# The first batch's q and k loaded by pairs of heads, and the global keys moved to the end of a key tile

## The chip, the cores and the metric

The kernel runs on one core of a Trainium2 chip. The metric is the time of one execution on the device in microseconds (us). Five engines work side by side, each through its own list of instructions in order: PE (matrix multiply, with its weight loads), DVE (vector), ACT (scalar, with tables for exp and sine), POOL (which here builds masks and issues most loads) and SP (which only issues DMAs). Semaphores tie the lists together. Results of PE land in PSUM, eight banks of 128 partitions by 512 f32, and DVE or ACT must carry them out before a bank is used again.

## The reference

Two layers, one after the other, on 4 batches of 768 positions, 8 heads of 64.

```python
scores = scale * np.matmul(q, k.transpose(0, 1, 3, 2))
is_global = pos[None, :] < 8
is_local = (rel >= 0) & (rel < 96)            # rel = query position - key position
dist = np.where(is_global & ~is_local, 96.0, np.abs(rel))
scores = np.where(is_global | is_local, scores - slopes[h] * dist, -1e9)
x = softmax(scores) @ v                        # heads side by side: 768 x 512 for each batch
proj = x @ w_proj                              # 512 -> 1536: x1, x2, x3
y = x1 * irfft(rfft(x2) * filter_fft) * x3     # along the 768 positions
out = y @ w_out
```

So a query sees the 95 keys before it, itself, and the first 8 keys of the sequence.

## The kernel before

**Tiles.** Keys go in tiles of 112 (`KL`), with the 8 global keys beside them so that one 128-row matmul gives both. Before the change a tile has 128 rows: 0 to 7 hold the global keys, 8 to 15 nothing, 16 to 127 the 112 local ones (`LO` is 16). Seven tiles cover 768 positions; the last starts at 656 and repeats 16 keys of the sixth. A tile of keys is multiplied with the 208 queries that can see it (96 for the last). The seven tiles are worked in three groups (`GRP`): two, two and three. Heads are taken in pairs (`hp` 0 to 3), one on partitions 0 to 63 and one on 64 to 127.

**Attention of a batch** (`attention`, L900 on). q and k come by DMA with positions on the partitions (`load_rows`, `load_q`: one head's 64 values make a packet of 256 bytes, cast to f16 on the way). PE turns them (`turned`, L668), DVE or ACT copies them out to `QT` and `KT`, `global_keys` copies the 8 global columns into every tile. Then, for each group and pair: `scores` (PE, L711), exp (ACT, L739), the mask (DVE, L751). In batch 0 the distance bias is instead added by PE (`biases`, L698: small matmuls with `slope` and `dg`, `near`, `edge`), so that no mask is needed. `values` (PE, L769 and L774) multiplies with V, which has a column of ones for the sum; DVE takes the reciprocal (L799) and scales (`xn`, L793); PE turns `xn` (L815) to `xT`. For groups 1 and 2 of batch 3 the turns are DMA transposes on SP (`crossed`, L657).

**Second layer.** `gate` (L860) makes x1 and x3; the butterflies and `conv` (L934, L622, L959) project and do the transform along positions with small tables in three classes; L986 is the output projection, then L310 or L312 and a store on SP. The tables come from a sine pass of ACT (`tables`, L424), which needs the sine table loaded and the exp table loaded again behind it. `spectrum` (L558 on) prepares the filter.

**The start.** q tiles 0 to 2 and k tile 0 are loaded as f32 by SP and ACT (`first_tiles`) and turned as f32 (`turned32`, L635). The other tiles of batch 0 come by POOL's queue, one DMA for a tile: k, q, then V (`load_first`). The 16 global rows of V of batch 0 are a small load of their own, copied by DVE into the seven tiles (`first_rows`). PE first runs idle matmuls (L302) on zeros.

**What sets the order.** Every operation of the program is an `Op` with the engines that may do it. The string `ORDER` at the top is the schedule, written out: `83P2` is operation 83 on PE with its result in bank 2, `74A` operation 74 on ACT, `i17b0` seventeen idle matmuls in bank 0. Each engine gets its instructions in the order of the string, and the string also decides whether DVE or ACT does a copy. Nothing is rearranged at run time; an engine that waits holds up all behind it.

Of the kernel before, what the change touches and what calls it, by code (L numbers as in the profile page):

```python
# [9 lines left out]
F32 = mybir.dt.float32  # L10
# [7 lines left out]
NG = 8  # L18
# [22 lines left out]
4V 0S 1A 2S 3A 30V 9G 32A 31A 14V 13V 11V 10A 33V 22G 34V 23V 60A 62A 12V 27V 5V 65A 36G 39G 19S 35A 15V 25V 24G 63A  # L41
16V 40G 18V 42G 41G 59A 45G 28V 8V 26V 46G 48G 29A 47G i17b0 74P0 75V 61A 70P1 72P2 71V 68P3 69V 84P45 64A 106P0 76P1
37G 58A 92P67 73A 79A 78A 93P 88P23 77V 94P 85P 38G 108P1 89P 49G 86P 107A 66V 90P 95A 44G 43G 109V 112P0 113V 87A
110P1 111V 80P67 81P 82P 20V 91A 51G 67V 120P01 83A 114P45 121A 152P2 153V 50G 154P3 155V 118P67 158P0 115A 159V 119A
156P2 157V 17V 116P45 21V 117A 160P67 161A 162P23 163A 96P45 97V 98V 101P01 166P67 167A 164P45 122P23 52G 102V 103V
123V 127P01 104P6 124V 128V 53G 129V 7G 217P7 165A 105A 99P4 168P23 125P6 130P5 258G 100V 218A 126A 212P4 131A 173P01
137P5 132P6 169V 170V 171P2 213A 219V 220V 221A 174V 175V 176P7 138P3 259G 172A 357P0 214V 215V 133P2 134A 267G 266G
216A 224P6 177V 199V 198V 206V 139V 385P7 184P4 358A 55G 135V 255G 189P5 140A 141V 386V 179P7 225A 257G 355P3 256G
264G 226A 183P0 265G 359A 6A 353P1 191A 201V 143P5 227V 181A 136V 194P7 56G 57G 185A 200V 202V 356V 383P0 228V 229A
205V 260G 186A 354V 208V 230A 223V 361P23 145A 203V 196A 367P45 362A 364P67 384V 178P1 207V 148P0 365A 295P2 204V 360V  # L50
368A 180V 396P45 150A 296A 397A 390P67 209V 210V 211V 187V 363V 370P01 371A 391A 293P3 294A 270G 369V 291P2 280P0 366V
387P67 222V 292A 398V 388A 231V 232V 233V 234V 393P45 299P3 300A 394A 54G 281A 282P2 283A 429P1 273G 306P3 307A 278P6
279A 147P7 149A 286P2 372V 261S 235V 236V 272G 287A 389V 142P3 433P6 434A 271G 431P7 144A 263G 430A 485G 237V 373P45
262S 151V 268G 297P2 298A 240P6 484G 241A 182V 193P3 195A 374V 432V 238P2 239A 392V 243P6 244A 269G 375V 395V 378P01
486G 379V 380V 435P45 436A 487G 197V 438P23 439A 404P67 405V 146V 376P0 496G 406V 245P1 246A 377V 437V 581P4 284P5
285A 444P23 445A 441P67 442A 407P1 188P0 488G 582V 399P45 381P2 408A 440V 585P3 274G 190V 400V 401V 446V 583P0 382A
586V 252P67 254A 253A 275G 276G 495G 584V 402P1 403A 447P45 489G 490S 443V 613P7 614A 248P23 448V 494G 587A 249A 304P6
305A 452P01 410P7 250A 412A 500G 247V 712G 449V 450P2 453V 454V 425P6 451A 251V 501G 455P3 659P7 456V 502G 427A 493G
302V 660A 595P01 589P45 498G 478V 590A 596A 592P23 593A 588A 414P6 458P7 499G 727G 468P4 416A 301V 661P5 308V 711G
460A 303V 242V 729G 594V 409P0 657P1 658V 611P2 309V 288V 612A 289V 424P6 426A 428V 477V 479V 290V 411A 470A 662A  # L60
473P1 475A 420P7 422A 415P6 413V 312P4 480V 313A 320P5 725G 417A 324P1 472P0 321V 474A 669P23 325A 598P67 599A 523P4
481V 714G 510P1 670A 316P5 314P0 192V 511A 600V 672P23 621P67 317V 524A 715G 482V 812P1 315A 591V 673A 322P4 323A 622A
310P0 311A 813V 730G 814A 418V 419P5 318P1 319A 597V 506P4 507A 421V 491S 463P5 465A 624P67 618P01 619A 666P23 457P4
667A 519P5 674V 625A 483V 508P0 663P23 881S 615P67 713G 326V 327V 328V 329V 623V 330V 520A 664A 462P1 423V 509A 620V
720G 728G 497G 616A 521P5 492G 606P23 505G 333V 334V 464A 467P0 469A 522A 607V 601P67 466V 277G 602V 608V 459A 626V
350P1 810P5 514P0 665V 351A 716G 347P4 603A 503G 835S 671V 525P1 526A 348A 476V 344P2 717S 722G 811V 837S 504G 527P5
345A 515A 528A 617V 668V 632P67 331V 604P4 605A 678P23 532P0 633V 634V 533A 679V 512P5 513A 680V 332V 808P1 627P67
628V 882S 534P0 675P45 676V 609P2 809A 629V 535A 610A 635P1 335P3 677V 630P2 631V 529V 636A 721G 836S 471V 336A 724G
530V 883S 821P01 822A 818P67 819A 820V 815P45 816A 726G 880S 723G 838S 516V 338P3 839V 652P2 654A 681S 339A 642P6 644A
817V 648P7 531V 846P45 517V 682S 840P23 683S 650A 847A 518V 823V 824P01 825A 826V 647P6 841A 643P7 645A 638P4 640A  # L70
719G 827P01 828V 884V 341P5 829V 342A 649A 646V 653P7 849P01 850A 536V 732G 537V 461V 651V 705V 891P45 343S 892A
888P23 704V 851V 637P6 544P0 689P1 707V 639A 655A 545A 548P4 731G 691A 549A 550P6 542P5 893V 842V 540P7 543A 706V 352S
538P0 539A 552P1 553A 695P4 551A 641V 700P0 541A 702A 708V 697A 690P1 830P67 546P0 692A 848V 685P4 684P1 831V 832V
889A 687A 843P23 693V 890V 709V 885P67 340S 547A 844A 894P45 733P0 895A 886A 554V 710V 896V 718S 750P2 855P45 856V
748P3 735P6 337S 686A 656V 857V 751A 845V 833S 834S 887V 555A 556V 699P2 736A 557V 734A 749A 852P45 853V 900P67 901V
897P01 349S 902A 854V 898V 899V 694P3 558V 737P4 754P5 746P0 738A 741P4 858S 755A 561V 747A 562V 752P1 903S 753A 742A
739P5 559V 560V 759P0 760A 761P6 762A 346S 757V 763V 740A 743V 859S 575P1 576A 701A 572P4 573A 696A 578P0 566P1 764V
904S 703V 871P2 756V 865P3 867A 563P4 564A 758V 771P3 767P5 567A 579A 861P6 772A 863A 744V 860P4 745V 769P7 779P3 780A
905S 765P6 775P0 768A 927V 773P1 926V 929V 688V 862A 928V 776A 568S 930V 931V 777P3 770A 778A 698V 937P5 569P4 766A
932V 774A 781V 782V 783V 946P7 784V 785V 933P6 947A 938A 935P7 936A 961P5 570A 948P3 941P7 949A 934A 786V 950P4 787V  # L80
788V 951A 939P3 906P6 942A 940A 571S 952P4 944V 959P7 960A 943V 577S 945V 954P1 955A 864V 870P3 962A 963V 875P7 964V
907P1 909A 953A 580S 957V 956V 916P5 917P0 919A 876P4 873A 908A 958V 872A 874V 790P1 877V 565S 791A 965P6 866P2 966A
969P3 970V 971P6 878A 879V 868A 789V 972A 574S 984P4 985A 967P7 978P2 968A 973V 980P6 981A 982P4 983A 918V 920V 793P7
869V 910V 796P6 979A 986V 922P2 974A 975V 797A 987A 921P3 799P6 800A 801S 923A 976V 977V 798S 794A 802P4 988V 805P6
991V 989V 795S 911P7 992V 912P3 924A 806A 990V 993V 925V 807S 792S 994V 1004V 1001P6 803A 913A 1006V 804S 914V 998P7
999A 1000S 915V 1007V 995P3 1005V 1011P7 1002A 1003S 1012V 996A 997S 1008P6 1014P3 1015A 1009V 1013S 1010S 1016S
"""


# [108 lines left out]

class Fused:
    PERIOD = 40.0  # L200
    NEAR = 3
    PAIR_X = ()
    PAIR_AB = ()
    PAIR_EO = ()
# [1044 lines left out]
```

## Time and profile before

| what | us |
|---|---|
| median of 3 runs (lowest to highest) | 169.65 (169.21 to 169.74) |
| profiled execution | 168.69 |
| its span | 166.8 |
| PE, DVE, ACT, POOL busy | 160.3, 152.9, 144.9, 73.6 |
| PE: idle matmuls | 1.19 to 7.68 |
| first exponential / last of batch 0 ends | 11.63 / 22.28 |
| first matmul with V | 18.51 |
| sine table load | 25.49 |
| first gate / first projection of the second layer | 25.39 / 37.53 |
| end of the last stretch of matmuls on the chain | 160.69 |

How to read it: times are from the start of the span of one profiled execution. The profile gives busy time of each engine, the time it sat idle and what ended that, and a chain of waits that is followed back from the last instruction. Matmuls overlap, so a busy PE can still have room: the spacing of their starts tells what they cost. A DVE or ACT instruction in a row of others also starts some 0.07 to 0.1 us before the one ahead is reported done.

### The profile page before, as it was taken

How to read it: one execution, taken by the hardware profiler on the slowest of the kernel's cores; microseconds unless marked ns; L12 is line 12 of the kernel's file. 1: busy time of each engine (PE TensorE's matmuls, PEld its weight loads, DVE VectorE, ACT ScalarE, POOL GpSimd, SP SyncE). 2: the span in 40 equal slices, each digit the busy share in tenths (PEclk: the TensorE clock that was granted, in tenths of full speed). 3: DMA queues.
4: the chain of work that ended last, by engine and by line, in shares of the span. 5: the costliest groups of instructions: out<-in, count | busy, mean ns of one | idle time of the engine just before them, and what ended most of it. 6: DMA issues, size and time to landing. Idle time of an engine off the chain costs nothing.

```text
span 166.8 us, 4251 instructions
## 1 busy us (share of the span) xinstructions
PE 160.3 (96%) x1621; PEld 99.8 (60%) x1621; DVE 152.9 (92%) x336; ACT 144.9 (87%) x302; POOL 73.6 (44%) x99
## 2 busy tenths in 40 slices
PE   7999999999999999999999989999999999999990
PEld 2566787664567876666457746765744844575430
DVE  5898979999999999999999979999999999999950
ACT  4589979999999998999999998999896788696731
POOL 7999999973889934999570000000000000000000
PEclk9999999999999999999999999999999999999999
DMA  5999999999999999999999990804052104300685
GB/s 121 193 141 127 130 171 166 169 208 181 169 164 154 155 150 63 92 140 149 158 157 130 125 130 19 265 5 118 17 132 51 63 4 181 137 0 0 246 317 194
DMA packets 92916, 22.06 MB, mean 132 GB/s; under 512 B 85760, under 2 KB 89824, under 8 KB 92896
## 3 DMA queue, kind: packets, MB, share of 16 engines
q0 software_dynamic: 75952, 11.95, 100.9%
q1 hardware_dynamic: 14864, 9.33, 23.9%
q10 hardware_dynamic: 2080, 0.52, 1.7%
q8 instruction: 12, 0.20, 0.5%
q14 instruction: 8, 0.07, 0.1%
HBM read 24.94 MB, written 6.29 MB: 187 GB/s over the span
## 4 chain that ended last, share of the span: by engine, by line
PE 58%; DVE 33%; issue 4%; DMA 3%; ACT 0%; DVEq 0%; SPq 0%
PE bank L860 15%; PE bank L986 9%; DVE E L751 8%; PE bank L934 6%; PE bank L959 4%; PE bank L302 4%; DVE xn L793 4%; PE bank L698 3%; DMA KT<-kn 3%; PE bank L711 3%; PE bank L668 3%; PE bank L622 3%; PE bank L769 2%; DVE g L871 2%; PE bank L774 2%
## 5 line engine op out<-in xcount | busy, mean ns | idle before, releaser
L860 PE MATMUL bank<-xT,w 128*128 128x384 f16 x256 | 47.9, 326 | 0.0
L739 ACT ACTIVATE E<-bank 128x832 f16<-128x832 f32 (+2 forms) x64 | 42.8, 759 | 1.1 <-PE bank L711 1.0
L860 PEld LDWEIGHTS <-w 128*128 128x128 f16 x256 | 23.6, 98 | 15.4 <-issue 0.7
L322 POOL DMA_DIRECT2D kn<-in_k_dram x27 | 22.5, 848 | 6.7 <-PE bank L668 4.8
L322 POOL DMA_DIRECT2D vn<-in_v_dram x28 | 24.0, 865 | 2.2 <-DMA w<-in_moe_w_proj_dram 0.9
L986 PE MATMUL bank<-wo,y 128*128 128x512 f16 x96 | 22.9, 379 | 0.1
L751 DVE TENSOR_TENSOR E<-E,mask 128x832 f16<-128x832 f16 (+1 forms) x36 | 21.7, 622 | 0.0
L322 POOL DMA_DIRECT2D qn<-in_q_dram x21 | 18.8, 904 | 3.5 <-PE bank L934 3.2
L310 ACT ACTIVATE ot<-bank 128x512 f32<-128x512 f32 x22 | 12.8, 615 | 5.9 <-PE bank L986 3.8
L793 DVE TENSOR_TENSOR xn<-bank,rc 128x512 f16<-128x512 f32 (+1 forms) x22 | 16.8, 766 | 0.6 <-DVE rc L799 0.2
L310 ACT ACTIVATE ab<-bank 128x512 f16<-128x512 f32 x24 | 14.6, 655 | 1.2 <-PE bank L934 1.2
L869 ACT CAST g<-bank 128x384 f16<-128x384 f32 x30 | 14.5, 523 | 1.2 <-PE bank L860 1.2
L769 PEld LDWEIGHTS <-E 128*128 128x128 f16 x224 | 14.0, 97 | 2.3 <-issue 0.4
L769 PE MATMUL bank<-vn,E 128*128 128x65 f16 x224 | 15.3, 193 | 0.0
L310 ACT ACTIVATE x<-bank 128x384 f16<-128x384 f32 x26 | 13.5, 528 | 2.0 <-PE bank L860 1.3
L986 PEld LDWEIGHTS <-y 128*128 128x128 f16 x96 | 9.1, 98 | 10.1 <-DVE y L1066 0.2
L774 PE MATMUL bank<-vn,E 128*128 128x65 f16 x192 | 15.1, 193 | 0.0
L711 PE MATMUL bank<-QT,KT 64*128 64x208 f16 (+1 forms) x224 | 14.0, 244 | 0.9 <-DVE KT L306 0.7
L306 ACT CAST X<-bank 128x512 f16<-128x512 f32 x24 | 14.2, 643 | 0.3 <-PE bank L622 0.2
L306 ACT CAST eo<-bank 128x384 f16<-128x384 f32 x29 | 13.4, 542 | 0.3 <-PE bank L962 0.3
L774 PEld LDWEIGHTS <-E 128*128 128x128 f16 x192 | 13.2, 97 | 0.5
L711 PEld LDWEIGHTS <-KT 64*128 64x128 f16 x224 | 8.7, 94 | 6.4 <-issue 2.5
(148 smaller groups left out, 337.4 us busy)
## 6 DMA issues: line engine op xcount, KB each, us to landing
out_dram<-ot SPq DMA_DIRECT2D x24, 256.0 KB, 2.4
vn<-in_v_dram POOLq DMA_DIRECT2D x28, 112.0 KB, 5.4
kn<-in_k_dram POOLq DMA_DIRECT2D x27, 112.0 KB, 5.2
qn<-in_q_dram POOLq DMA_DIRECT2D x21, 128.0 KB, 5.6
w<-in_moe_w_proj_dram POOLq DMA_DIRECT2D x4, 256.0 KB, 5.7
g<-in_moe_filter_fft_dram POOLq DMA_DIRECT2D x1, 768.0 KB, 10.2
ot<-in_q_dram ACTq DMA_DIRECT2D x2, 256.0 KB, 6.6
w<-in_moe_w_proj_dram POOLq DMA_DIRECT2D x1, 512.0 KB, 7.2
```

The source lines that it names most:

```text
L306: {"A": nc.scalar.copy, "V": nc.vector.tensor_copy, "G": nc.gpsimd.tensor_copy}[e](out, in_)
L310: self.nc.scalar.mul(out, in_, c)
L322: return self.g.op(eng, 0.57 + 0.00035 * nbytes[0] if eng == "G" else 0.5, lambda _: e.dma_start(dst, src), w=w, r=r, nbytes=nbytes, name= ...
L711: nc.tensor.matmul(bs[hh].f32()[:, off:off + w], self.KT[hs, hp, P * m:P * m + P], self.QT[hs, hp, KL * m:KL * m + w], start=(off == 0 and ...
L739: nc.scalar.activation(dst, src(), Act.Exp, scale=self.scale)
L751: g.op("V", dve(w, 2), lambda _: nc.vector.tensor_mul(eo, eo, mk), r=[("mask", 2 * hp), ("mask", 2 * hp + 1)], w=[("E", hp, gi)], name="ma ...
L769: nc.tensor.matmul(o[:, n, hh], ef[:, at:at + P], vt[:, t, 2 * hp + hh, 0:D + 1], start=first, stop=(t == 0), skip_group_check=True)
L774: nc.tensor.matmul(o[:, n, hh], ef[:, at:at + P], vt[:, t - 1, 2 * hp + hh, 0:D + 1], start=False, stop=True, skip_group_check=True)
L793: nc.vector.tensor_mul(to, o[:, :, :, 0:D].rearrange("p i (t h) d -> p i t h d", h=2), rc.rearrange("p i (t h) o -> p i t h o", h=2).to_br ...
L860: nc.tensor.matmul(bk.f32()[:, 0:h], self.w[:, c, o + P * j:o + P * j + P], self.xT[:, c, h * s:h * s + h], start=(c == 0), stop=(c == 3))
L869: first = g.op("AV", {"A": act(h), "V": 0.0005}, lambda e: nc.scalar.copy(x3, pts[1].f32()[:, 0:h]) if e == "A" else None, use=[pts[1]], w ...
L986: nc.tensor.matmul(bk.f32(), y[:, c, P * t:P * t + P], self.wo[:, c, :], start=(c == 0), stop=(c == 3))
```

## The change

Three things and a new order:

- **First q and k.** In batch 0 q and k are loaded by pairs of heads. A partition gets six positions one after the other (`h (p i) d -> p h (i d)`, i = 6), so a packet has 1536 bytes instead of 256. Pairs 0 and 1 come as f32 by SP (q) and ACT (k), pairs 2 and 3 as f16 by POOL. DVE packs each (768 values on a partition, heads side by side) into `h1` or `h2`, which are free at that time. Six matmuls against the identity with 56 columns (positions 0 to 335) and six with 72 (336 to 767) turn a pair; they write every sixth column of a bank, which puts the positions back in order. The copies out are 336 or 432 columns for q; for k, 336 columns in three tiles and, in the second half, 96 more for the last tile; the 8 global columns are copied once for each pair. Scores of a pair can begin when that pair has come.
- **Key tiles.** A tile now has its 112 keys in rows 0 to 111 and the global keys in 112 to 119. The last tile starts at 672 and has 96. So the turns of k and `xn` have 112 or 96 columns instead of 128, the zero fills of `kn` go, and `dg` (with the masks of it) is 208 columns wide instead of 304. Corrections of `dg` and `far` are made on rows 96 to 127 with numbers for each row (`kf`).
- **Global V rows of batch 0** come as in the other batches: by two DMAs on SP from the first rows of V's first tile, once that has landed. `first_rows` goes.
- **The order** is new throughout. Idle matmuls are 10 instead of 17, the angles of the sine tables stand in front, V is asked for right behind the pairs. More of the `xT` copies are on DVE (13 of 16 instead of 5), more pieces of `xn` on ACT (44 instead of 20).

```diff
-    NEAR = 3
+    PLAIN = (0, 1)
+    NEAR = (0, 1, 2, 3)
+    CUT = (0, 336, 768)
...
-        self.K0 = [KL * t for t in range(6)] + [S - KL]
+        self.K0 = [KL * t for t in range(7)]
+        self.KW = [min(KL, S - x) for x in self.K0]
...
-        lo, hi = self.K0[t], self.K0[t] + KL
-        self.load("G", dst[P - (hi - lo):P, t, :, 0:self.D],
+        lo, hi = self.K0[t], self.K0[t] + self.KW[t]
+        self.load("G", dst[0:hi - lo, t, :, 0:self.D],
...
+    def load_pair(self, what, hp):
+        src = (self.q if what == "q" else self.k)[0, 2 * hp:2 * hp + 2].rearrange("h (p i) d -> p h (i d)", i=6)
+        key = ("first", what, hp)
+        if hp in self.PLAIN:
+            x = 2 * self.PLAIN.index(hp) + (what == "k")
+            self.rows[what, hp] = self.otp.rearrange("p a b -> p (a b)")[:, 768 * x:768 * x + 768].rearrange(
+                "p (h n) -> p h n", h=2)
+            return self.load("S" if what == "q" else "A", self.rows[what, hp], src, [key], (256, 1536), f"{what}hp{hp}")
+        buf, x = self.qn if what == "q" else self.kn, 1024 * (hp - len(self.PLAIN))
+        self.rows[what, hp] = buf.rearrange("p t h d -> p (t h d)")[:, x:x + 768].rearrange("p (h n) -> p h n", h=2)
+        return self.load("G", self.rows[what, hp], src, [key], (256, 1536), f"{what}hp{hp}")
...
-        ng = LO if b == 1 else NG
+        ng = LO if b < 2 else NG
...
-            self.load("S", vt[0:ng, t:t + n], vt[LO:LO + ng, 0:1].to_broadcast(
+            self.load("S", vt[KL:KL + ng, t:t + n], vt[0:ng, 0:1].to_broadcast(
...
+    def turned_pair(self, what, hp):
...
+        g.op("AV", {"A": act(n), "V": dve(n, 2 if plain else 4) + (0 if plain else 0.05)}, lambda e: self.copy(
+            e, packed, rows.rearrange("p h (i d) -> p i h d", i=6)), r=[("first", what, hp)] + (
+            [("ot", i) for i in range(6)] if plain else [(what + "n", t) for t in range(6 if what == "q" else 7)]),
+            w=[key], name="pack")
+        for x in range(2):
+            lo, hi = self.CUT[x], self.CUT[x + 1]
+            n, p0 = (hi - lo) // 6, lo // 6
+            b = g.bank()
+
+            def turn(_, b=b, n=n, p0=p0):
+                o = b.f32()[:, 0:6 * n].rearrange("p (c i) -> p c i", i=6)
+                for i in range(6):
+                    nc.tensor.matmul(o[:, :, i], flat[:, P * i:P * i + P], self.ident[:, p0:p0 + n],
+                                     start=True, stop=True, skip_group_check=True)
...
+            def put(e, b=b, x=x, kv=kv):
+                self.copy(e, kv[:, 3 * x:3 * x + 3, 0:KL], b.f32()[:, 0:3 * KL].rearrange("p (t c) -> p t c", t=3))
+                if x:
+                    self.copy(e, kv[:, 6, 0:self.LAST], b.f32()[:, 3 * KL:3 * KL + self.LAST])
...
+                    nc.tensor.transpose(b.f16()[:, 512 * x + P * i:512 * x + P * i + m],
+                                        buf[0:m, t, 2 * i:2 * i + 2, :], self.ident[0:m, 0:m])
...
             for i in range(4):
-                self.scores(i, c, b == 0 and c < self.NEAR)
+                if b == c == 0:
+                    for what in "qk":
+                        self.turned_pair(what, i)
+                self.scores(i, c, b == 0 and i in self.NEAR, b == 0)
...
-        self.first_rows(vt)
         self.distances()
-        for c in range(3):
-            for t in ([], [3, 4], [5])[c]:
-                self.load_q(0, t)
-            for t in ([1], [2, 3], [4, 5, 6])[c]:
-                self.load_run(("kn",), self.kn, self.k, t, 1)
-            for t in self.GRP[c]:
-                self.load_run(("vn", 0), vt, self.v, t, 1)
+        for hp in range(4):
+            if hp not in self.PLAIN:
+                for what in "qk":
+                    self.load_pair(what, hp)
+        for t in range(7):
+            self.load_rows(("vn", 0), vt, self.v, 0, t)
+            if t == 0:
+                self.load_global(vt, 0, LO)
```

The start of the new order, beside that of before (`...` where it goes on):

```diff
-4V 0S 1A 2S 3A 30V 9G 32A 31A 14V 13V 11V 10A 33V 22G 34V 23V 60A 62A 12V 27V 5V 65A 36G 39G 19S 35A 15V 25V 24G 63A
-16V 40G 18V 42G 41G 59A 45G 28V 8V 26V 46G 48G 29A 47G i17b0 74P0 75V 61A 70P1 72P2 71V 68P3 69V 84P45 64A 106P0 76P1
...
+4V 0S 1A 2S 3A 26V 15G 17V 10V 16G 18V 19G 20V 9G 21V 22V 23V 52A 53A 51A 57A 11V 7G 55A 13V 33G 28V 8V 35G 27V 32G
+i10b0 216P0 24V 66V 34G 54A 61V 58A 56A 25V 217A 12V 221P1 222A 223V 218V 36G 80V 31V 219V 93V 75V 106V 29V 37S 42G
...
```

## Prediction

> **What bounds the kernel now.** I read the page first (engine table, then the chain of waits), then the timeline of the first 40 us, then the stretches of the end. The page:
>
> ```profile
> span 166.8 us, 4251 instructions
> ...
> PE 160.3 (96%) x1621; PEld 99.8 (60%) x1621; DVE 152.9 (92%) x336; ACT 144.9 (87%) x302; POOL 73.6 (44%) x99
> ...
> PE 58%; DVE 33%; issue 4%; DMA 3%; ACT 0%; DVEq 0%; SPq 0%
> ```
>
> Three engines are nearly full, and the chain that ends last lies on PE and DVE, never on ACT. The chain in order of time says where it changes hands:
>
> ```profile
> 1.19 6.49 PE bank L302 x17
> 7.68 1.75 PE bank L635 x16
> ...
> 35.73 0.69 DVE QT L306
> ...
> 93.17 5.37 DMA KT<-kn
> ...
> 157.29 3.40 PE bank L986 x16
> 160.69 1.90 issue
> ```
>
> PE opens with 17 idle matmuls, then DVE carries the chain from 35.7 to 93.1, a DMA transpose of keys follows, and from 98.8 to 160.7 PE runs without a hole. What I compare at are these points of the timeline of each engine:
>
> ```profile
> 11.63 3.13 ACT L739 ACTIVATE E<-bank 128x832 f16<-128x832 f32 x4 [0.32 <-PE bank L711]
> 11.81 6.48 POOL L322 DMA_DIRECT2D vn<-in_v_dram  x7
> 18.51 0.24 PE L769 MATMUL bank<-vn,E 128*128 128x65 f16 x2
> 25.49 1.28 ACT L424 ACT_TABLE_LOAD   x1
> 37.53 1.03 PE L934 MATMUL bank<-w,xcf 128*128 128x512 f16 x4
> 38.97 1.59 DVE L751 TENSOR_TENSOR E<-E,mask 128x832 f16<-128x832 f16 x3
> ```
>
> The first exponential starts at 11.63, the first values matmul at 18.51 (V is only asked for from 11.81), the first projection at 37.53. I count PE work by the spacing of starts in the timeline: 0.217 us for 512 columns, 0.163 for 384, 0.109 for 256, 0.055 for 128, 0.030 for 65, half for the 64-row score and bias matmuls, which run in pairs. Behind 18.51 this gives 137.7 us, against 142.2 us that pass to 160.69. Behind 37.53 it is 120.1 of 123.2. So PE has about 3 us of holes after the front: time is won only by reaching the projections earlier or with less PE work left.
>
> The profiled execution took 168.69 us (span 166.8 and 1.9 around it), 0.96 below the median of 169.65 and outside the three runs (169.21 to 169.74). I work out a difference on the span and put it on the median.
>
> **Part 1, start of PE.** Ten idle matmuls instead of 17. The early ones start every 0.427 us, twice the later spacing, so ten end near 1.19 + 4.27 = 5.46. The angle matmuls come next (512, 512, 256, 256 columns, at the slow spacing 0.43 + 0.43 + 0.21 + 0.21 and two tiny ones): about 6.9. The slow spacing ends near 6.3 in the trace; if it ended with the idle ones, the angles would be 0.6 shorter.
>
> **Part 2, first q and k.** Four 393 KB loads on SP's and ACT's queues. With two such queues and 256-byte packets this trace moves 285 GB/s between 3 and 4 us; 2 KB store packets at the end reach 381. The first pair (786 KB) needs 2.1 to 2.8 us after the first bytes at about 2, so it lands at 4.5 to 5.0. DVE's 24 instructions ahead of the first pack sum to about 4.4 us from 0.86 (idle 0.27, masks' edges, near copies 0.14 to 0.69, gaps 0.27, ones 0.10 + 0.27), so it is there at 5.3: DVE, not the load, decides. A plain pack of 768 f32 is three quarters of the 1024-element cast (0.673): 0.5. k and q of pair 0 are packed at 6.3, ahead of PE's 6.9. Six turns of 56 or 72 columns: 0.18 to 0.20 us (65 columns take 0.030); 96 of them are 3.0 us against 16 fp32 transposes (1.75) and 36 f16 ones (2.0) removed. The strided PSUM write is not in the trace: nothing extra (as the 65-column row) to double, +3.0 us of PE; I take nothing, since in this stretch PE waits for ACT.
>
> **Part 3, ACT's front.** Table load after the distances (POOL: iota 0.31 and two selects 0.79 from 0.9, DVE's corrections to 2.6; the load itself 1.28, to 3.9), eight masks of 208 instead of 304 columns (spacing 0.36 for 304; estimate 0.28) to 6.2, two angle passes (0.62, 0.39) to 7.4. Then, in ACT's new order, up to the sine table: twelve sets of exponentials (10.65 us in the trace, 11.63 to 22.28) and some 18 evacuations and copies (0.42 for 336 columns from the 384 row at 0.45, 0.50 for 432, 0.20 for 96, 0.23 for the global copy): 15.9 us in all, ending at 23.3. The table load is thus 2.2 us earlier than 25.49 although the exponentials end 1 us later: the angles are done beforehand and the first xT copies come only behind the table.
>
> **Part 4, V.** POOL issues 11 loads for batch 0 instead of 16: four pair loads (0.70 each: 0.82 for 896 rows, 0.77 for 512) from 4.2, then V from 7.0 instead of 11.81. Behind them come batch 1's loads and the weights; the filter, which DVE needs from 41.2, is reached at 27.0 instead of 29.63, 10.2 from landing, so it stays ahead of its use. Batch 1's k and q loads now wait for the packs of pairs 2 and 3 (done by 12.0; POOL gets there at 11.9 and 13.6). The first V tile lands near 11.5 (4.5 median in that stretch). Removed on DVE: two 16-partition V copies (0.67 and 1.42) and the zero fills of keys and rows (1.12, 0.48, 0.48), which had cover. Added: batch 0's global V rows now go by two copies on SP, behind nothing on SP but the two q loads, but waiting for V's first tile; batch 1's two such copies stand behind them and have until 48, its first reciprocal of values.
>
> ```profile
> vn<-vn SPq DMA_DIRECT2D x1, 120.0 KB, 6.6
> vn<-vn SPq DMA_DIRECT2D x1, 48.0 KB, 5.6
> ```
>
> These are the same copies in batch 1, beside V loads: 5.6 us. Beside nothing the nearest row is 2.4 (a store). So landing at 14.0 to 18.8, taken at 17.1 by the 5.6 row, as V loads again run beside it. PE wants the first values at about 16.6 by ACT's order; behind them in PE's order stand the scores of pair 3, wanted by ACT at 18.1. Stall of PE 0.5, of ACT almost none; bounds 0 and 1.5. The Trainium skill (DMA: Bandwidth & Descriptors, Anatomy of one DMA) puts a DMA at about 2.0 us plus bytes over 436 GB/s: 2.1 us for 48 KB, an estimate by a fit made for the GpSimd path; by it there is no stall and the sum below would be 0.3 less, 168.7. The same page (Issuing engines are not separate DMA queues) says all queues share 16 engines and interleave, which speaks for the slow row.
>
> **Part 5, later batches.** Key turns of 112 (or 96) columns save 0.006 to 0.013 us on each of 64, x turns the same on 72: 1.1 us of PE in all. The last key tile brings 96 rows instead of 112 per load. The five transposes of keys by DMA keep their place on SP; their global columns no longer follow them on DVE (one 0.19 copy on the chain goes). The order moves work between DVE and ACT: ten 448-column xT copies on DVE instead of three (0.38 each), 24 more 64-column xn pieces on ACT (0.2 each) instead of three on DVE (0.68). The second exp table load has no dummy in front and now waits for batch 1's first scores: 0 to 1.28; by my walk the scores are done at 28.0 and ACT comes at 28.3, so 0.
>
> **Sum.** I follow the new orders from these times to the first projection, row by row with the durations of the trace less the 0.08 to 0.1 that neighbours overlap. DVE: packs and angles done at 12.0, seven copies out of banks (3.3) at 15.3, one mask (1.1) at 16.4, then two masks' and six xn's worth of batch 0 with the turns of batch 1 between them, full from 22.4 to 28.3, then 23 instructions (butterflies 0.34 to 0.47, q and k copies 0.27 to 0.6) of 8.6. ACT: 23.3, table 1.28, sines 0.9, copies of KT and xT 2.2 and inverse tables 0.5 to 28.3, exp table 1.28, four exponentials 3.1, two x, four g and two table copies 3.4, two exponentials more 1.5. PE waits for the ninth of these (x, 36.05). So PE: reaches it at 36.1 to 36.5 instead of 37.53 (it waits for ACT's x copy), but has 121.4 us left instead of 120.1 (more of batch 0's gates are postponed): between -0.1 and +0.3. DVE: first masked E at 36.9 instead of 38.97, with 0.5 more left: -1.6. ACT: first evacuation of a projection at 37.6 instead of 38.59, 0.9 more left: -0.1. Part 4's stall adds 0.3. The chain lies on DVE first and PE afterwards, so I take the middle of the two, -0.75, plus 0.3, rounded to -0.6: span 166.2, execution 168.1, median 169.0.
>
> **The rivals.**
> - *Global V rows come late (slower).* Place: the first values matmul on PE. For it: two DMAs in series, 4.5 to 5.5 and 5.6 to 6.6, and an issue of 0.6. If V lands at 12.5 and the copy 7.2 later, PE stands from 16.6 to 19.7; ACT has 1.5 us of scores in banks, so 1.6 reach it and everything behind: -0.9 without the stall, + 1.6 = +0.7, 170.4. It decides from a landing at about 18. Against it: DMA packets of q and k are larger and may leave the queues empty.
> - *ACT's front is longer than its sum (slower).* Every turn waits for a bank which ACT must clear, and ACT waits for the turn; a dozen handovers at 0.1 to 0.2 us beyond what I counted put the exponentials' end at 25.0. Then ACT's first projection evacuation is at 39.3 with 0.9 more to do, and PE at 37.9 with 1.3 more: +1.6 by both, 171.2. It decides from 0.7 us of such waits. For it: ACT is 87% busy overall but full between 11.6 and 22.3, and gets 5 us of work there. Against it: ACT is not on the chain of before.
> - *PE keeps its lead (faster by more).* The first values at 16.6 instead of 18.51 with 0.4 more left is -1.5, and if DVE's -1.6 is passed on, holes do not grow: 167.7.
> - *Nothing.* The front's lead is used up by the postponed gates: 169.6.
>
> **How the numbers follow.** Forecast 0.30, PE keeps its lead 0.15, nothing 0.12, late V rows 0.23, longer ACT front 0.20. A measurement here tells 0.3% (0.5 us) from no change. Faster 0.45, same 0.12, slower 0.43. The range runs from 167.0 (the fast rival with PE's holes down by 0.7) to 171.8 (the ACT rival with half of the table load's bound, 0.6); the forecast's own is 168.2 to 169.2.
>
> **What would show it.** First exponential at 9.6 (wrong if after 10.5); exponentials' end at 23.3; V's copies landing at 17.1 and no PE wait over 1 us for DMA at the first values; first projection at 36.1 to 36.5; PE without holes from about 98. The prediction is wrong if the first gates come after 29.5, if DVE waits between 36 and 95 for more than the 0.8 us it waits now for a key transpose, or if PE's turns take twice 0.030.

## The result and the profile after

The change makes the kernel slower, by a little over 1%. In the first comparison, both kernels on one chip, the changed kernel took 171.34 us (median of four runs, 171.2 to 172.03) against 169.69 us (four runs, 169.21 to 169.74): a ratio of 1.0112, 95% interval 1.0079 to 1.0145. A second comparison on another occasion gave 171.45 against 169.32 us, 1.0139 (1.0106 to 1.0172). The forecast was 169.0 us, faster by 0.6; the time lies inside its range, on the other side of no change. Where a median and a ratio below tell different things, the ratio is the one to read, since it goes by all undisturbed executions and not by the middle one.

The profiled execution of the changed kernel took 172.03 us, the slowest of its four, while that of the kernel before (168.69) lay below all of its own. Their difference, 3.3 us, is about twice that of the medians, so this page shows where the time goes better than how much of it. The page of the changed kernel, the lines that answer to those of before (span, engines, the chain's shares):

```profile
span 170.3 us, 4366 instructions
...
PE 162.8 (96%) x1658; PEld 101.1 (59%) x1658; DVE 155.6 (91%) x350; ACT 147.7 (87%) x323; POOL 67.6 (40%) x93
...
PE 78%; DVE 12%; DMA 3%; ACT 2%; issue 2%; SPq 0%; ACTq 0%; DVEq 0%
```

PE is 2.5 us busier, and its share of the chain rises from 58% to 78%, at DVE's cost. The chain in order of time (start, duration, what) says with what:

```profile
7.30 0.82 DVE h L311
8.16 2.02 PE bank L654 x18
...
15.82 2.79 PE bank L654 x48
...
154.00 4.33 PE bank L1016 x20
158.35 0.61 ACT ot L315
...
159.35 2.35 DMA out_dram<-ot
...
162.80 2.91 DMA out_dram<-ot
```

L654 is the turns of batch 0's q and k. Two stretches of them, 2.02 us for 18 and 2.79 us for 48, lie on the chain where the kernel before had a 1.75 us run of transposes and two of 0.55. At the end the chain leaves PE and passes twice through a store of an output (L315 is the copy out of a bank, then its DMA). The kernel before passes through none: there PE's matmuls run to the last copy. The points of the timeline (start, duration, engine, line) by which the prediction compared:

```profile
7.71 5.10 POOL L327 DMA_DIRECT2D vn<-in_v_dram  x6
12.33 0.86 ACT L770 ACTIVATE E<-bank 128x832 f16<-128x832 f32 x1
14.03 1.40 SPq L327 DMA_DIRECT2D vn<-vn  x2
20.88 0.24 PE L800 MATMUL bank<-vn,E 128*128 128x65 f16 x2
27.31 1.28 ACT L422 ACT_TABLE_LOAD   x1
39.38 1.89 PE L964 MATMUL bank<-w,xcf 128*128 128x512 f16 x8
41.08 2.93 DVE L782 TENSOR_TENSOR E<-E,mask 128x832 f16<-128x832 f16 x5
```

Every point of the front but the issue of V's loads is later than before: first exponential 12.33 (11.63), first values 20.88 (18.51), sine table 27.31 (25.49), first projection 39.38 (37.53), first masked E 41.08 (38.97). V is asked for 4.1 us earlier (7.71 against 11.81) and yet its first use is 2.4 us later. Waits that the kernel before did not have stand in the list of waits (who waited, for whom, us in total, times, longest):

```profile
ACT QT L311 <- PE bank L654: 2.3, 3, 0.8
DVE QT L311 <- PE bank L654: 1.9, 2, 1.6
DVE ot L317 <- DMA out_dram<-ot: 1.8, 1, 1.8
ACT KT L311 <- PE bank L654: 1.5, 2, 0.8
ACT ot L315 <- DMA out_dram<-ot: 1.4, 2, 1.2
```

ACT and DVE, which were to be the busy ones of the front, stand 5.7 us in all for turns; and at the end they stand 3.2 us for output buffers whose stores are under way.

### The profile page after: what moved, and what is told of

Its sections match the earlier page's. It is cut to its first block, busy times and chain, and to the rows that moved or that the text cites. A ratio compares the mean times of both kernels' runs of the same rounds, so it can differ in the third digit from the quotient of the medians.

```text
span 170.3 us, 4366 instructions
## 1 busy us (share of the span) xinstructions
PE 162.8 (96%) x1658; PEld 101.1 (59%) x1658; DVE 155.6 (91%) x350; ACT 147.7 (87%) x323; POOL 67.6 (40%) x93
## 3 DMA queue, kind: packets, MB, share of 16 engines
q0 software_dynamic: 67552, 11.54, 89.7%
## 4 chain that ended last, share of the span: by engine, by line
PE 78%; DVE 12%; DMA 3%; ACT 2%; issue 2%; SPq 0%; ACTq 0%; DVEq 0%
PE bank L892 21%; PE bank L964 11%; PE bank L1016 9%; PE bank L743 6%; PE bank L989 5%; PE bank L654 4%; PE bank L628 4%; PE bank L800 4%; PE bank L730 4%; PE bank L805 3%; DMA out_dram<-ot 3%; PE bank L702 3%; PE bank L847 1%; DVE xn L824 1%; PE bank L992 1%
## 5 line engine op out<-in xcount | busy, mean ns | idle before, releaser
L892 PE MATMUL bank<-xT,w 128*128 128x384 f16 x256 | 48.7, 326 | 0.5 <-DVE x L317 0.5
L770 ACT ACTIVATE E<-bank 128x832 f16<-128x832 f32 (+2 forms) x64 | 44.0, 774 | 0.3 <-PE bank L743 0.2
L892 PEld LDWEIGHTS <-w 128*128 128x128 f16 x256 | 23.6, 98 | 16.9 <-issue 2.0
L327 POOL DMA_DIRECT2D vn<-in_v_dram x28 | 23.2, 845 | 7.7 <-PE bank L702 6.6
L1016 PE MATMUL bank<-wo,y 128*128 128x512 f16 x96 | 22.4, 379 | 0.4 <-DVE ot L317 0.4
L327 POOL DMA_DIRECT2D qn<-in_q_dram x20 | 17.8, 895 | 4.7 <-DMA g<-in_moe_filter_fft_dram 3.0
L327 POOL DMA_DIRECT2D kn<-in_k_dram x23 | 18.8, 827 | 2.1 <-DMA w<-in_moe_w_proj_dram 1.1
L315 ACT ACTIVATE ot<-bank 128x512 f32<-128x512 f32 x21 | 12.5, 617 | 6.1 <-PE bank L1016 4.6
L315 ACT ACTIVATE ab<-bank 128x512 f16<-128x512 f32 x24 | 15.7, 653 | 1.8 <-PE bank L964 1.5
L901 ACT CAST g<-bank 128x384 f16<-128x384 f32 x30 | 15.4, 543 | 0.5 <-PE bank L892 0.4
L311 ACT CAST X<-bank 128x512 f16<-128x512 f32 x24 | 14.9, 651 | 0.4 <-PE bank L628 0.4
L824 DVE TENSOR_TENSOR xn<-bank,rc 128x512 f16<-128x512 f32 (+1 forms) x19 | 14.8, 784 | 0.4
L315 ACT ACTIVATE x<-bank 128x384 f16<-128x384 f32 x26 | 13.4, 528 | 0.2
```

What stands on the lines that cost most here:

```text
L311: {"A": nc.scalar.copy, "V": nc.vector.tensor_copy, "G": nc.gpsimd.tensor_copy}[e](out, in_)
L315: self.nc.scalar.mul(out, in_, c)
L327: return self.g.op(eng, 0.57 + 0.00035 * nbytes[0] if eng == "G" else 0.5, lambda _: e.dma_start(dst, src), w=w, r=r, nbytes=nbytes, name= ...
L770: nc.scalar.activation(dst, src(), Act.Exp, scale=self.scale)
L824: nc.vector.tensor_mul(to, o[:, :, :, 0:D].rearrange("p i (t h) d -> p i t h d", h=2), rc.rearrange("p i (t h) o -> p i t h o", h=2).to_br ...
L892: nc.tensor.matmul(bk.f32()[:, 0:h], self.w[:, c, o + P * j:o + P * j + P], self.xT[:, c, h * s:h * s + h], start=(c == 0), stop=(c == 3))
```

## The experiments

All runs, by what reached PE and DVE in each profiled execution (starts in us) and by the time. The ratio is to the kernel before on the same chip, with its 95% interval.

| run | edit | first values | first projection | first masked E | us | ratio |
|---|---|---|---|---|---|---|
| before | none | 18.51 | 37.53 | 38.97 | 169.69 | 1 |
| after | the change | 20.88 | 39.38 | 41.08 | 171.34 | 1.0112 (1.0079 to 1.0145) |
| after2 | the change again | 19.99 | 38.50 | 39.89 | 171.45 | 1.0139 (1.0106 to 1.0172) |
| i14 | 14 idles | 19.40 | 37.90 | 39.28 | 171.16 | 1.0087 (1.0050 to 1.0123) |
| flat | turns flat | 19.91 | 38.41 | 39.79 | 171.31 | 1.0096 (1.0061 to 1.0131) |
| v0 | V first | 19.57 | 38.26 | 39.65 | 170.51 | 1.0101 (1.0066 to 1.0137) |
| i14flat | 14 idles, turns flat | 19.73 | 38.22 | 39.60 | 171.03 | 1.0066 (1.0030 to 1.0101) |
| i14v0 | 14 idles, V first | 18.38 | 36.90 | 38.29 | 169.41 | 0.9998 (0.9971 to 1.0025) |
| flatv0 | turns flat, V first | 17.53 | 36.68 | 38.07 | 169.50 | 1.0007 (0.9978 to 1.0036) |
| front3 | all three | 17.48 | 36.82 | 38.20 | 169.17 | 0.9997 (0.9976 to 1.0018) |
| ot12 | 12 output buffers | 20.32 | 38.81 | 40.20 | 171.08 | 1.0101 (1.0061 to 1.0140) |
| best | three (q's turns only), 12 buffers | 17.52 | 36.86 | 38.25 | 168.92 | 0.9987 (0.9964 to 1.0010) |
| iq | best without the buffers | 17.54 | 36.73 | 38.13 | 169.70 | 1.0023 (0.9988 to 1.0058) |
| b_i10 | before, 10 idles | 19.43 | 38.53 | 39.98 | 169.22 | 0.9993 (0.9962 to 1.0024) |

The first theory was that the front lost the time in three places at once: PE starts slowly, its turns are twice as long as assumed, and V's copied rows come late; and that the stores at the end add some. The rivals: one of these alone, or none, with the loss behind the front.

**One cause at a time.** i14 and b_i10 change the number of idle matmuls in the hand-written order, in the new and the old kernel:

```diff
-i10b0 216P0 24V 66V 34G
+i14b0 216P0 24V 66V 34G
```
```diff
-29A 47G i17b0 74P0 75V
+29A 47G i10b0 74P0 75V
```

> The changed kernel with 14 idle matmuls instead of 10, nothing else. In the profile of the changed kernel PE is idle from 5.71 to 6.60 and from 7.68 to 8.16, and everything up to about 13.5 is spaced twice as wide as later: the first 18 turns take 2.02 us (0.112 each), the later ones of the same 56 and 72 columns 0.058. Theory A (the slow spacing lasts because the idle matmuls end before PE's work is ready): 14 at 0.427 end at 7.0 to 7.4, the first hole is closed, the first 18 turns take 1.1 us and the first exponential starts near 11.1 instead of 12.33; if the delay goes through the front as a whole, 170.2 to 170.7 instead of 171.3. Theory B (DVE's packs and the handovers between PE and ACT set the pace of the front): the first exponential moves, but the last one of batch 0 ends at 27.0 or later as now (27.3), and the time stays within 0.4 of 171.3. If the wide spacing comes from the strided writes or from cold buffers, the 18 turns still take 2.0.

> The kernel before with 10 idle matmuls instead of 17, nothing else: one part of the change by itself. Theory A (the slow spacing lasts until PE has worked without a hole for some us): the wide spacing, which ends near 6.3 in the kernel before, lasts to 9.5 or later, its 16 first transposes take up to 3.5 instead of 1.75 us, the first exponential starts 0.8 to 1.8 later than 11.63, and the time is 170.2 to 171.3 instead of 169.7. Theory B (the spacing follows the time since the start, or the front has slack for it): first exponential within 0.4 of 11.63, time 169.4 to 170.0.

In i14 the timeline of PE and the first exponential:

```profile
8.17 1.31 PE L654 MATMUL bank<-ident,h 128*128 128x56 f16 x18 [0.87 <-DVE h L311]
10.88 0.88 ACT L770 ACTIVATE E<-bank 128x832 f16<-128x832 f32 x1
13.91 2.85 PE L654 MATMUL bank<-ident,h 128*128 128x56 f16 x48
```

The 18 turns take 1.31 us instead of 2.02 and the first exponential comes 1.45 earlier: theory A for the mechanism. The sine table starts at 25.82 instead of 27.31 and the first projection at 37.90 instead of 39.38. But the ratio, 1.0087, lies within the interval of the changed kernel's: the time goes as theory B said, though not by B's own sign, since the exponentials end before 25.82 and not at 27.0 or later. In b_i10 the kernel before gets the same slow start by the same edit:

```profile
7.00 3.02 PE L635 MATMUL bank<-p,ot 128*128 128x128 f32 x16 [1.98 <-DMA ot<-in_k_dram]
12.56 1.62 ACT L739 ACTIVATE E<-bank 128x832 f16<-128x832 f32 x2 [0.64 <-PE bank L711]
```

Sixteen transposes take 3.02 instead of 1.91 us in that view, the first exponential starts 0.93 later and the first projection 1.00 later, as theory A says; and the time does not move (0.9993). The list of PE's waits from 37 us on says why. Before:

```profile
PE bank L711 <- DVE KT L306: 0.7, 1, 0.7
```

In b_i10 this line is gone; the weight load ahead of it waits 0.4 us where it waited 1.1. The kernel before came early to the keys that are transposed by DMA near 93 us and waited for them; that a front later by 1.0 lost only 0.3 of span (167.1 against 166.8) fits the 0.7 that was waited there anyway. A later front need not be paid one for one.

**The turns.** flat lets each turn write neighbouring columns of the bank instead of every sixth:

```diff
-                o = b.f32()[:, 0:6 * n].rearrange("p (c i) -> p c i", i=6)
+                o = b.f32()[:, 0:6 * n].rearrange("p (i c) -> p i c", i=6)
                 for i in range(6):
-                    nc.tensor.matmul(o[:, :, i], flat[:, P * i:P * i + P], self.ident[:, p0:p0 + n],
+                    nc.tensor.matmul(o[:, i], flat[:, P * i:P * i + P], self.ident[:, p0:p0 + n],
```

> The changed kernel, with the turns of batch 0's q and k writing each its own run of 56 or 72 neighbouring fp32 columns of the bank instead of every sixth column. The copies out of the bank are left as they are, so q and k of batch 0 come out in six-token order: that part of the computation is changed, the work is the same in count and size. Theory A (a strided write to the bank doubles the turn): the 48 turns that take 2.79 us from 15.82 (0.058 each) take 1.4 to 1.5 (0.030), PE has 2.7 us less work in the front, the exponentials of batch 0 end at 25.3 to 26.3 instead of 27.3, and the time is 169.9 to 170.6. Theory B (a turn of so few columns has a floor near 0.058, for its weights change with every one): the 48 turns still take 2.8 and the time is 171.0 to 171.6. If turns are short but ACT was not waiting for them, 2.7 us of PE go and the exponentials still end after 27.0.

The same 48 turns in flat's timeline, then the first values, and the row of the granted clock:

```profile
15.15 1.77 PE L654 MATMUL bank<-ident,h 128*128 128x56 f16 x48
...
19.91 0.22 PE L800 MATMUL bank<-vn,E 128*128 128x65 f16 x2 [0.80 <-DMA qn<-in_q_dram]
```
```profile
PEclk9956999999999999999999999999999999999999
```

1.77 us against 2.85 in the same view of the changed kernel (i14's line above has the same 2.85): 0.037 per turn on the mean against 0.059. The 1.77 still holds five slow turns at its start and a pause of 0.13; from start to start a flat turn takes 0.026 for 56 columns and 0.032 for 72, a strided one 0.049 and 0.062. The strided write is what doubles the turn. Again the time hardly moves: PE now stands 0.80 us at the first values for a DMA. The trace names the q loads there; the work that it waits for, as the next runs show, is the copy of V's global rows, issued in this run at 13.45 and 6.3 us from landing.

The clock row shows half and 0.6 of full speed in the third and fourth of 40 slices, 8.5 to 16.9 us, where this run's spacing is wide until about 15. Its first two slices stand at 9 although the idle matmuls there start every 0.43 us, and in the changed kernel's own page the row is 9 throughout although its spacing is just as wide until 13.5, so the spacing of equal matmuls is the better witness. It fits the Trainium skill (TensorE: Matmul & The Clock Gate, Part 1: The HAM clock gate): the array runs at half clock until one free-running window of about 3.4 us has been busy, so where the work falls in the window decides. This case fits that, as far as it goes (no run shows where the window lies): ten idles end at 5.71, PE then stands 0.9 us for POOL and DVE and 0.5 for the first pack, and pays the wide spacing for 8 to 9 us more.

**The end.** ot12 lays six more output buffers over the rows of k and q, which the last batch no longer needs:

```diff
             o = self.outs % 6
+            if last:
+                o = (6, 7, 8, 9, 10, 11)[t]
             self.outs += 1
+            extra = [] if o < 6 else [("kn" if o < 9 else "qn", 2 * (o % 3) + x) for x in range(2)]
```

> The changed kernel with six further output buffers, laid over those of k and q rows, for the six outputs of the last batch; nothing else. In the profile of the changed kernel the last copies out of banks wait 1.4 to 1.8 us three times for output buffers whose stores are still under way, and the last one ends at 166.4. Theory A (these waits end last): they vanish, the end comes 0.5 to 0.9 us sooner, 170.4 to 170.8. Theory B (the twelve stores themselves, or the projections on PE, end last whatever the buffers): the waits vanish and the time stays within 0.3 of 171.3.

The waits for stores are gone, and PE's 0.4 us for a bank with them. The time, 171.08, is within 0.3 of 171.3, as theory B said; the interval is too wide to exclude a gain of 0.5. See iq below.

**V's rows, and all three.** v0 moves one token of the order on GpSimd's queue; front3 is v0 with the edits of i14 and flat. best writes only q's turns flat, and lets the copy out of the bank put them in order:

```diff
-13V 33G 28V 8V 35G 27V 32G
+13V 36G 33G 28V 8V 35G 27V 32G
```
```diff
-                    e, self.QT[:, hp, lo:hi], b.f32()[:, 0:hi - lo]), use=[b],
+                    e, self.QT[:, hp, lo:hi].rearrange("p (c i) -> p c i", i=6),
+                    b.f32()[:, 0:hi - lo].rearrange("p (i c) -> p c i", i=6)), use=[b],
```

> The changed kernel once more, unedited, to have its time beside the others on this chip. 171.0 to 171.6. If the wide spacing of PE's first instructions changes from execution to execution, its first exponential lies elsewhere than 12.33, between 10.9 and 12.4, and the whole front moves with it.

> The changed kernel with the load of V's first tile asked for ahead of the four loads of q and k pairs 2 and 3 on GpSimd's queue (at 4.72 instead of 7.71), nothing else. The two copies of the global rows, which wait for that tile, should be issued at 10.5 to 11.5 instead of 13.4 to 14.4 and land near 17 instead of 19.4 to 20.4. Theory A (three things end last together in the front: the slow spacing, the strided turns, V's copies): alone it gains little, 0 to 0.4, since PE comes to the first values at about 20 anyway: 170.8 to 171.4. Theory B (V's copies alone decide): first values at 18.5 to 19.0 and 169.7 to 170.3. Theory C (q and k of pairs 2 and 3, 0.8 later, are wanted at once): 171.6 to 172.2.

> The changed kernel with the three edits of the front together: 14 idle matmuls, turns of batch 0 that write neighbouring columns (q and k of batch 0 stay in six-token order, so that part of the computation is changed), V's first tile asked for first. Theory A (the front decides, and these three are what it lost): first exponential 10.3 to 10.9, 48 turns in 1.4 to 1.7 us, first values matmul at 17.9 to 18.6 instead of about 20.3, first masked E at 37.8 to 38.5 instead of 40.2 to 41.1, and the time 168.8 to 169.7, as the kernel before. Theory B (the loss lies behind the front, in the order of later work): the front moves as said but the time stays above 170.3. Theory C (ACT or DVE, not PE, bounds the stretch from 20 to 39): the first values move by 2 and the first masked E by less than 0.8.

> A version that computes all of it: the changed kernel with 14 idle matmuls, V's first tile asked for first, the turns of q alone written to neighbouring columns (the copy out of the bank then reads every sixth group and writes in order; k keeps its strided turns), and six further output buffers laid over the rows of k and q for the last batch. Theory A: the front gains 0.6 us less than with all turns flat, the tail 0.3 to 0.6: 168.7 to 169.6, against 169.4 for the kernel before. Theory B (the loss lies behind the front): above 170.2. If the strided read out of the bank costs as the strided write did, ACT's copies of 336 columns take 0.8 instead of 0.44 and the first values come at 19.5 or later.

after2's front came about 1 us earlier than in the first profile, 38.50 at the first projection with the same first turns (1.98 us): the slow start varies, but all six profiled executions of the new kernel with ten idle matmuls have it, until some time between 11 and 15 us. v0 issues V's copies at 9.19 instead of 13.5 to 14.0. Its first values come at 19.57, later than theory B had them, its median of 170.51 lies between the two theories. But its seven executions fall into two groups (170.2 to 170.5 and 171.5 to 171.8), so the median says little, and its ratio, 1.0101, does not tell it from the changed kernel: whatever it gains alone is less than the loss. front3 goes as theory A said, with first values even earlier (17.48 against 17.9 to 18.6) and the time of the kernel before. Its copies are issued from 8.68; its first values:

```profile
17.48 0.24 PE L800 MATMUL bank<-vn,E 128*128 128x65 f16 x2
```

Three edits that take off 0 to 0.9 us of the median each alone take off 2.3 together (171.45 to 169.17), all that the change had lost. best, which computes everything, is at 168.92, 2.5 below the changed kernel; against the kernel before, 0.9987 with an interval that holds 1, it is no faster that can be told. Its strided read costs nothing: up to 24 us ACT's three copies of 432 columns of q take 528 ns on the mean with it, 521 in after2 and 525 in i14v0, which both read in order; DVE's three of 336 take 497, 507 and 496.

**Which pairs.** The three pairs tell how the causes hang together.

> The changed kernel with 14 idle matmuls and V's first tile asked for first; the turns stay strided. Two of the three front edits, whose sum took 2.3 us off. If the three causes wait on one another (taking one away lets PE run into the next), the pair without the flat turns lies between: the 48 turns take 2.8 us, first exponential 10.2 to 10.6, first values 18.2 to 18.9, first masked E 38.6 to 39.2, 169.7 to 170.2. If flat turns carry the whole gain, 170.4 or more; if they carry none, 169.0 to 169.4.

> The changed kernel with flat turns (q and k of batch 0 stay in six-token order, so that part of the computation is changed) and V's first tile asked for first; 10 idle matmuls as in the changed kernel. If the slow start of PE costs by itself: wide spacing to 12 or later, first exponential 10.8 to 11.5, first values 18.2 to 19.0, 169.6 to 170.2. If V's early tile and flat turns carry all, 169.0 to 169.4.

> The changed kernel with 14 idle matmuls and flat turns (q and k of batch 0 stay in six-token order, so that part of the computation is changed); V's first tile keeps its place behind the four loads of pairs 2 and 3. The last of the three pairs. Theory A (V's copied rows are a floor under the first values): the copies are issued near 13.5 and land at 19.2 to 20.0, PE stands up to 1.5 us at the first values for a DMA, first masked E at 39.3 or later, 170.5 to 171.2 although PE has no slow start and no strided turns. Theory B (any two of the three edits bring nearly the whole gain): first values at 17.5 to 18.4 and 169.2 to 169.7, as the other two pairs.

Either pair with V first has the whole gain (0.9998, 1.0007), more than the half-way that was expected of them. The pair without it has not (1.0066, its interval above 1): theory A of the last run. PE's waits in i14flat, and where the first of them lies in its timeline:

```profile
PE bank L654 <- DVE h L311: 2.4, 4, 0.9
PE bank L800 <- DMA qn<-in_q_dram: 1.7, 1, 1.7
```
```profile
13.71 1.40 SPq L327 DMA_DIRECT2D vn<-vn  x2
```
```profile
19.73 0.22 PE L800 MATMUL bank<-vn,E 128*128 128x65 f16 x2 [1.71 <-DMA qn<-in_q_dram]
```

The copy of V's global rows is issued at 13.71, 5.9 us from landing, so it is there at 19.6, and PE, ready at 18.0, starts at 19.73. Where V is asked for first (front3, flatv0) the copies are issued at 8.7 to 9.0 and this wait is gone. So there were two limits close to one another: V's copies held the first values at 19.3 to 20.3 (issue and landing in i14, flat, ot12, i14flat and the changed kernel), and PE with its slow start and its long turns came there at 19.6 to 20.9. Taking away only one shows the other. With V early, one of the two PE edits is enough, since then the exponentials on ACT are next: the sine table starts at 24.61 to 24.83 in i14v0, flatv0 and front3 alike, whichever PE edit they have, and ACT's waits between 9 and 27 us sum to 0.8 to 1.1 there, against 3.8 in the changed kernel.

The edit that asks for V first does one thing more than its expectation says. In all six runs with it DVE's third and fourth packs start 0.8 us earlier (9.77 to 9.81 and 11.54 to 11.58, against 10.55 to 10.58 and 12.32 to 12.35), and PE's turns wait for packs. From i14flat to front3 the first values move by 2.25 us; 1.71 of it is the wait for the DMA, and the other 0.5 can be the packs. No run moves one without the other, so what each is worth in time is not shown.

**The buffers again.**

> The version called best, without its six further output buffers: what the buffers are worth where the front is no longer in the way. First values as there (17.5) and first masked E at 38.2 to 38.3. Theory A (the waits for output stores end last): 169.2 to 169.6, 0.3 to 0.6 above best's 168.9, with the last copies waiting 1.2 to 1.8 for stores. Theory B (the stores end last whatever the buffers): within 0.2 of 168.9.

169.70 against best's 168.92: the direction and size of theory A, and iq still has the wait `DVE ot <- DMA out_dram<-ot` (1.9 us) that best lacks. But the intervals (0.9988 to 1.0058, 0.9964 to 1.0010) overlap, and iq's profiled execution, at 171.28, lies 1.6 above its median (one of the twelve took 907.87, unexplained), so what the buffers are worth stays open between 0 and 0.8. iq is also i14v0 with q's turns flat: its first values come 0.84 earlier (17.54 against 18.38), yet at 1.0023 against 0.9998 it is no faster. With V first and 14 idles in, flat turns gain nothing that can be told.

## Why the prediction was wrong, by its own steps

- **Part 1, start of PE: wrong.** Taken: the angles end at about 6.9 and the wide spacing ends near 6.3 or with the idles. Measured: the angles end at 7.68, and the spacing is wide until about 13.5 in the profile of the changed kernel and 15 in flat, because the seven idles that were removed leave PE standing for DVE and POOL. b_i10 shows the same price in the old kernel: 1.0 us of front.
- **Part 2, the first pack and the turns: the term mis-sized most.** The turns take 0.049 to 0.062 at full speed, the upper of the two bounds given (0.030 to double); "I take nothing" was the failed choice, and its reason ("in this stretch PE waits for ACT") was false: ACT and DVE waited 5.7 us for PE's turns. A rule that speaks against the change was there to be read: the Trainium skill (SBUF — State Buffer, Door 1: The DMA port swizzle) says that any non-contiguous access to PSUM significantly slows matmuls. flat agrees: 1.77 against 2.85 us for 48 turns. By the time alone the term does not show: flat is no faster than the changed kernel until V's rows are early too. The first pack started at 7.30, not 5.3: DVE's instructions ahead of it ended there, and the two loads of k, issued from 0.80, have a median of 6.2 us to landing (for those of q the profile gives none), so they too come near 7.0 and not at 4.5 to 5.0. The pack took 0.82, not 0.5. So the first exponential, forecast at 9.6 and called wrong after 10.5, came at 12.33 and 12.23.
- **Part 3, ACT's front: the work right, its start and the waits wrong.** Sine table predicted 23.3, measured 27.31 and 26.43 in the changed kernel, 24.75 in front3. The forecast was 15.9 us of work from 7.4, the end of the angle passes. In front3 these end at 8.70, since they wait for PE's angle matmuls; then ACT works for 14.9 us and waits for 1.2. In the changed kernel's profile they end at 8.11, the work is 15.3 and the waits are 3.9. Front3's angle passes:

```profile
7.83 0.87 ACT L413 ACTIVATE y<-bank 128x512 f32<-128x512 f32 x2 [1.07 <-PE bank L444]
```

- **Part 4, V: wrong, and the mechanism was a rival.** The copies were put at 17.1, with bounds of 14.0 to 18.8, from a first V tile landing at 4.5 us after its issue. Behind four pair loads on the queue it took about 6 (copies issued at 13.5 to 14.5 after an issue at 7.71); asked for first, the 4.5 held (4.72 to 9.19 in v0). They landed at 19.3 to 20.3, beyond the 18 from which the rival "Global V rows come late" decides. The sign named, no PE wait over 1 us for DMA at the first values, held in the first profile only because PE itself was late; i14flat shows 1.71. The row of 5.6 us for the copy itself was right (5.7 to 6.3). The Trainium skill's fit in the prediction (DMA: Bandwidth & Descriptors, Anatomy of one DMA) gave 2.1 us for 48 KB as an estimate; here such a copy took 5.5 to 6.8 in every run, beside other loads, so the row of the trace decides.
- **Sum.** PE's work left behind the first projection, counted again in the way of the prediction, is 121.5 against 120.3 us: the 1.3 more was right within 0.2. With the measured first projection the account of PE alone holds: after2 has 38.50 - 37.53 = +0.97, and 1.2 of work more, together +2.2; measured 171.45 - 169.32 = +2.1. It holds less well where the front is early: front3 gives -0.71 + 1.2 = +0.5 where the medians say -0.15, with an interval of 0.35 on either side. What failed in the sum is the step "the chain lies on DVE first and PE afterwards, so I take the middle of the two": DVE's first masked E came 1 to 2 us later than before, not 2 earlier, and the chain went over to PE. Even front3's front, 0.7 earlier at the projections, is no gain in time; the postponed work is enough to take it back. Two slips of arithmetic come on top. -0.75 plus 0.3 is -0.45, not -0.6. And the 3 us of holes came from setting the work up to the last matmul against the time to 160.69, where the kernel before still has matmuls to run (below). To the last of these there are about 4.5 us of holes behind the first projection, and about 5 in after2 by the same count: there was more to win by closing holes than the prediction said.

```profile
157.13 5.38 PE L986 MATMUL bank<-wo,y 128*128 128x512 f16 x24
```

- **The end: not in the sum.** "PE without holes from about 98" failed by 0.4 to 0.5 us, and the last copies wait for stores. Both orders have twelve outputs at the end over six buffers. In the kernel before the first six are stored from 154.93 to 157.59 and the next six copies start at 159.11. In the new order the first six are copied from 155.19 on, but stored only from 158.97 to 162.43, since SP's list has the store of the fourth copy first, and the next six copies come from 161.80. No run changed the order of the stores. It stands in none of the rivals.
- **The rivals.** The time, 171.3 to 171.45, is the one that "ACT's front is longer than its sum" gave (171.2). Its sign, the first gates after 29.5, came true (31.73 in the first profile), but the handovers of ACT were the smaller part: PE's turns, its slow start and V's rows made ACT wait, and without them the loss is gone. "Nothing", the front's lead used up by postponed gates, is what front3 would be. The sign on key transposes did not come: DVE does not wait for one between 36 and 95 us.

What stays open is why the changed kernels still need 128.9 to 129.6 us from the first masked E to the end where the kernel before needs 127.8 (iq's disturbed profile left aside): 1.1 is PE's work left there (120.0 against 118.9 us by the same count), new waits of 0.5 for a copy of x and 0.5 at the last outputs come on top, and the old 0.7 for keys goes. best, which lacks the 0.5 at the last outputs, is the one with 128.9; no run took the rest apart.

## What to carry to other kernels

Price a matmul's output pattern as well as its columns: here a write to every sixth fp32 column cost nearly as much as twice the columns, while a strided read by the copy out of the bank cost nothing, so put the permutation there. When work is taken off a start-up, check what kept PE busy until its clock was up, and follow a load that others are queued ahead of to its landing and through whatever copies it. If removing a clear cause moves the local points but not the time, look for a second limit close behind the first and remove them in pairs.

## What was not expected of the hardware

The same DVE instruction took two durations, depending on the order of the loads on GpSimd's queue. DVE in the changed kernel, where GpSimd issues the pair loads from 4.72 and V's tiles from 7.71:

```profile
5.92 0.40 DVE L317 TENSOR_SCALAR eo<-ident 64x128 bf16<-64x128 f16 x1
...
7.30 1.65 DVE L311 CAST h<-ot 128x768 f16<-128x768 f32 x2
```

and in v0, where one V tile is issued first and the pair loads follow until 8.6:

```profile
5.93 0.19 DVE L317 TENSOR_SCALAR eo<-ident 64x128 bf16<-64x128 f16 x1
...
7.17 1.07 DVE L311 CAST h<-ot 128x768 f16<-128x768 f32 x2
```

Same operands, 0.40 against 0.19 and 1.65 against 1.07. All six profiles with the pair loads first have 0.39 to 0.41 and 1.64 to 1.66, all six with V's tile first 0.19 and 1.06 to 1.07, so that the order of the loads decides is shown. The Trainium skill (SBUF — State Buffer, Who interferes with whom) says that DVE's two-port modes and GpSimd exclude one another for a whole instruction. The traces fit that, but no view shows the one waiting for the other, so this mechanism is argued and not shown. v0's first turns start 0.37 earlier (7.79 against 8.16), behind the quicker packs.
